# GpSimd takes a subtraction and a product of the query softmax in the first eight units of an attention and token mixer

## The chip, the cores and the metric

The kernel runs on one core of a Trainium2 chip. The metric is the device time of one execution in microseconds (us), as the median of several runs; lower is better. A core has a matrix engine (TensorE, PE in the profile), a vector engine (VectorE, DVE), an activation engine (ScalarE, ACT), a general engine (GpSimd, POOL) and a queue that issues transfers (SyncE, SP). Each runs its own instructions in the order in which they stand in the program, and waits on semaphores for the others.

## The reference, cut to what matters

Shapes: batch 8, 8 heads, 576 positions, head size 64, model size 512, 256 token features, 1536 channel features, all float32.

```python
q_s = exp(q - max(q, axis=-1)); q_s = q_s / (sum(q_s, axis=-1) + 1e-9)
k_s = exp(k - max(k, axis=2));  k_s = k_s / (sum(k_s, axis=2) + 1e-9)
kv  = einsum('bhsd,bhse->bhde', k_s, v)
x   = einsum('bhsd,bhde->bhse', q_s, kv)          # then (batch, 576, 512)
h   = relu(x^T @ w_tok1) @ w_tok2                 # mixes the 576 positions
u   = x + h^T
out = u + relu(u @ w_ch1) @ w_ch2                 # mixes the 512 channels
```

## The kernel before

**Units.** The attention and the token mixing are done in 32 units, one for each batch and each pair of heads (`n = b * 4 + j`). A unit's queries are one tile `q_t` of 128 partitions by 640 (five blocks of 128 positions, the last one half real, by two heads of 64). A unit goes through these steps: `softmax_k` and `softmax_q`; `stage_qT` (transposes of the queries on PE, L340 and L343); `stage_kv` (the product of keys and values, L310); `stage_y` (the queries times the first token weight, L375); `stage_h1` (L383, then `hh` on ACT at L390 and its low half `hl` on DVE at L391); `stage_u` (L428 and L412 on PE, then L416 on ACT and L417 on DVE empty the result).

**Early units.** Units 0 to 7 are "early": they come before the channel mixing starts, and they use tiles of a pool that holds three of each (`q_t` of unit n + 3 takes the place of that of unit n). The channel weights and token weights come as 64-bit numbers, and `narrow` turns each piece of 128 by 512 into float32 with five operations on DVE (L192, L194, L195, L197, L199) and one on ACT (L193); `split` then makes a high half on ACT (L117) and a low half on DVE (L118). That narrowing is the filling work of DVE among the early units: the token weights first, then four pairs of channel pieces.

**The query softmax, before.** DVE takes the maximum of each of the ten rows of 64 in a partition (L278). In units 0 to 3 (and 8 to 11) DVE negates it (L281) and ACT does ten exponentials of 64 with the maximum as bias, each of which also gives its sum (L284). In the other units DVE subtracts the maximum (L288), ACT does one exponential of 640 (L289), and DVE sums (L290). Then DVE adds 1e-9 (L291), takes the reciprocal (L292) and multiplies the whole tile by it (L293). For early units that is the end; late units go on to a high and a low half of the queries, the low one on GpSimd (L118).

**The main part.** From about 81 us on the channel mixing runs: for each of nine blocks of 512 positions, 12 steps of two big products (L488 and L648 on PE), with the late units between them.

**What sets the order.** The code gives the instructions in an order, and the compiler's scheduler then places them by its own estimate of when each engine is free, so that each engine's list is fixed when the program is built. A change to one operation can therefore move many others. Nothing is reordered while it runs.

Of the kernel before, what the change touches and what calls it, by code (L numbers as in the profile page):

```python
# [12 lines left out]
ALU = mybir.AluOpType  # L13
AX = mybir.AxisListType

P = 128
# [4 lines left out]
def attn_mixer_kernel(ctx: ExitStack, tc: tile.TileContext, q, k, kt, v, wt, out, dims):  # L21
# [3 lines left out]
    nc = tc.nc  # L25
    B, H, S, D, TOK, DM, DCH, wide = dims
    NJ = DM // P
# [8 lines left out]
    NE = 2 * NJ  # L36
# [75 lines left out]
    def f32(ap):  # L112
        return ap.bitcast(F32)

    def split(hi, lo, src, lo_eng):

        nc.scalar.copy(hi, src)  # L117
        return lo_eng.tensor_tensor(lo, src, f32(hi), op=ALU.subtract).ins  # L118
# [153 lines left out]

    def softmax_q(u):
        G = 2 * C1
        st = sm.tile([P, 3, G], F32, name="st")
        qc = u["q"]
        qt = qc.rearrange("p c (h d) -> p (c h) d", h=2)
        nc.vector.tensor_reduce(st[:, 0, :], qt, axis=AX.X, op=ALU.max)  # L278
        if u["n"] < NJ or NE <= u["n"] < NE + NJ:

            nc.vector.tensor_scalar(st[:, 0, :], st[:, 0, :], -1.0, None, op0=ALU.mult)  # L281
            for i in range(G):
                one = slice(i, i + 1)
                nc.scalar.activation(  # L284
                    qt[:, i, :], qt[:, i, :], AF.Exp, bias=st[:, 0, one], accum_out=st[:, 1, one]
                )
        else:
            nc.vector.tensor_tensor(qt, qt, st[:, 0, :].unsqueeze(2).broadcast_to([P, G, D]), op=ALU.subtract)  # L288
            nc.scalar.activation(qc, qc, AF.Exp)  # L289
            nc.vector.tensor_reduce(st[:, 1, :], qt, axis=AX.X, op=ALU.add)  # L290
        nc.vector.tensor_scalar(st[:, 1, :], st[:, 1, :], 1e-9, None, op0=ALU.add)  # L291
        nc.vector.reciprocal(st[:, 2, :], st[:, 1, :])  # L292
        nc.vector.tensor_tensor(qt, qt, st[:, 2, :].unsqueeze(2).broadcast_to([P, G, D]), op=ALU.mult)  # L293
        if u["early"]:
            return
        qh = wk.tile([P, C1, P], F32R, name="qh")
        ql = wk.tile([P, C1, P], F32R, name="ql")
        q_low[:] = [split(qh, ql, qc, nc.gpsimd)]

        nc.scalar.copy(qh[TL:P, C, :], f32(ql[TL:P, C, :]))  # L300
        u["qh"], u["ql"] = qh, ql
# [393 lines left out]
    def soft(n):  # L695
        if n < NU:
            softmax_k(units[n])
            softmax_q(units[n])
# [21 lines left out]
    early = early_pools.enter_context(tc.tile_pool(name="early", bufs=NB))  # L720
# [88 lines left out]
    for n in range(NE, NU):  # L809
# [13 lines left out]
        if n + 1 < PAIRED:  # L823
            put(at, lambda n=n: after(drained, softmax_k, units[n + 1]))
            put(at, lambda n=n: after(drained, softmax_q, units[n + 1]))
            put(at + 1, lambda n=n: after(drained + q_low, exp_k, units[n + 1]))
        elif n + 1 < NU:
            put(at, lambda n=n: after(drained, softmax_q, units[n + 1]))
# [15 lines left out]
    n = len(steps)  # L844
# [119 lines left out]
```

## Time and profile before

| what | value |
|---|---|
| time, three runs | 794.89, 797.23, 797.31 us; median 797.23 |
| profiled execution | 798.31 us, of which the span from first to last instruction is 796.5 us |
| mean granted TensorE clock | 0.994 |
| GpSimd work between 2.9 us and 111.6 us | none |

The profile is of one execution. A row of its timeline gives the start, the duration, the engine, the line, the operation and the tiles; consecutive instructions of one kind are merged, with their count. The recorded durations of DVE instructions overlap a little, so what an instruction costs its queue is read from the start of one to the start of the next.

### The profile page before, as it was taken

How to read it: one execution, taken by the hardware profiler on the slowest of the kernel's cores; microseconds unless marked ns; L12 is line 12 of the kernel's file. 1: busy time of each engine (PE TensorE's matmuls, PEld its weight loads, DVE VectorE, ACT ScalarE, POOL GpSimd, SP SyncE). 2: the span in 40 equal slices, each digit the busy share in tenths (PEclk: the TensorE clock that was granted, in tenths of full speed). 3: DMA queues.
4: the chain of work that ended last, by engine and by line, in shares of the span. 5: the costliest groups of instructions: out<-in, count | busy, mean ns of one | idle time of the engine just before them, and what ended most of it. 6: DMA issues, size and time to landing. Idle time of an engine off the chain costs nothing.

```text
span 796.5 us, 12193 instructions
## 1 busy us (share of the span) xinstructions
PE 781.0 (98%) x4478; PEld 651.9 (82%) x4478; DVE 526.9 (66%) x1224; ACT 331.9 (42%) x896; POOL 83.4 (10%) x72
## 2 busy tenths in 40 slices
PE   6899999999999999999999999999999999999997
PEld 5688888888888788888888888888888888888886
DVE  6889999876776445655575555563767458975440
ACT  6977554455643343243433434343434413332100
POOL 1000010011112111020200201111111000000020
PEclk8899999999999999999999999999999999999999
DMA  9754333324334221513132222212240000000011
GB/s 289 236 160 132 105 126 107 107 78 128 87 102 136 65 75 35 152 36 99 39 106 67 80 57 80 92 54 81 51 126 18 1 1 32 22 1 0 1 67 40
DMA packets 64276, 65.10 MB, mean 82 GB/s; under 512 B 41432, under 2 KB 44760, under 8 KB 64216
## 3 DMA queue, kind: packets, MB, share of 16 engines
q1 hardware_dynamic: 59608, 56.06, 23.9%
q10 hardware_dynamic: 4608, 8.26, 2.7%
q8 instruction: 35, 0.57, 0.3%
q14 instruction: 25, 0.20, 0.1%
HBM read 54.85 MB, written 9.45 MB: 81 GB/s over the span
## 4 chain that ended last, share of the span: by engine, by line
PE 94%; DVE 2%; DMA 1%; SPq 1%; ACT 1%; issue 0%; DVEq 0%
PE ps_o L648 33%; PE ps_h L488 29%; PE ps_h L597 7%; PE ps_h L375 6%; PE ps_h L412 6%; PE ps_h L648 4%; PE ps_h L310 2%; PE ps_h L458 2%; PE ps_h L383 2%; DMA kt_t<-in_kt 1%; PE ps_o L375 1%; PE ps_o L412 1%; PE ps_o L428 0%; DVE mc L241 0%; PE ps_h L428 0%; DVE stg L197 0%
## 5 line engine op out<-in xcount | busy, mean ns | idle before, releaser
L648 PE MATMUL ps_o<-h2h,cw 128*128 128x512 f32 x768 | 225.5, 391 | 0.0
L488 PE MATMUL ps_h<-uh,cw 128*128 128x512 f32 x672 | 210.1, 393 | 0.0
L648 PEld LDWEIGHTS ps_o<-h2h,cw 128*128 128x128 f32 x768 | 142.5, 188 | 29.8 <-DVE stg L685 0.5
L492 DVE SCALAR_TENSOR_TENSOR h2l<-ps_h,h2h 128x512 fp32r<-128x512 f32 x84 | 57.8, 689 | 152.6 <-ACT h2h L491 152.6
L488 PEld LDWEIGHTS ps_h<-uh,cw 128*128 128x128 f32 x672 | 123.7, 188 | 24.5 <-issue 0.5
L648 PE MATMUL ps_o<-h2l,cw 128*128 128x512 f32 x384 | 137.3, 391 | 0.0
L488 PE MATMUL ps_h<-ul,cw 128*128 128x512 f32 x336 | 131.0, 390 | 0.0
L648 PEld LDWEIGHTS ps_o<-h2l,cw 128*128 128x128 f32 x384 | 71.9, 188 | 15.3 <-DVE h2l L492 0.3
L118 POOL TENSOR_TENSOR ql<-q_t,qh 128x640 fp32r<-128x640 f32 x24 | 38.2, 1590 | 421.2 <-ACT qh L117 383.6
L491 ACT ACTIVATE h2h<-ps_h 128x512 fp32r<-128x512 f32 x84 | 50.0, 595 | 71.9 <-PE ps_h L488 70.8
L488 PEld LDWEIGHTS ps_h<-ul,cw 128*128 128x128 f32 x336 | 63.1, 188 | 13.4
L362 DVE COPY stack<-cv_s 32x160 f32<-32x160 f32 (+1 forms) x264 | 56.2, 231 | 3.6 <-PE ps_h L458 0.7
L270 POOL TENSOR_TENSOR k_t<-k_t,mb 128x640 f32<-128x640 f32 x24 | 38.2, 1590 | 119.4 <-DMA mb<-row 83.3
L271 ACT ACTIVATE k_t<-k_t 128x640 f32<-128x640 f32 x24 | 17.8, 741 | 72.1 <-POOL k_t L270 70.7
L506 DVE TENSOR_TENSOR ul<-ps_h,ul 128x512 f32<-128x512 f32 x40 | 27.5, 692 | 24.2 <-PE ps_h L597 23.9
L416 ACT CAST uh<-ps_h 128x128 fp32r<-128x128 f32 (+4 forms) x104 | 27.6, 288 | 30.7 <-PE ps_h L458 20.2
L362 ACT COPY stack<-cv_s 32x128 f32<-32x128 f32 (+1 forms) x120 | 36.9, 308 | 2.8 <-DVE cv_s L352 1.5
L417 DVE TENSOR_TENSOR ul<-ps_h,uh 128x128 fp32r<-128x128 f32 (+4 forms) x104 | 30.8, 312 | 6.0 <-ACT uh L416 5.1
L412 PE MATMUL ps_h<-w2h,hh 128*128 128x320 f32 (+1 forms) x112 | 33.7, 302 | 0.0
L412 PE MATMUL ps_h<-w2l,hh 128*128 128x320 f32 (+1 forms) x112 | 33.1, 298 | 0.0
L648 PE MATMUL ps_h<-cw 128*128 128x512 f32 x144 | 33.0, 389 | 0.0
L412 PE MATMUL ps_h<-w2h,hl 128*128 128x320 f32 (+1 forms) x112 | 32.6, 298 | 0.2 <-DVE hl L391 0.2
(249 smaller groups left out, 1283.8 us busy)
## 6 DMA issues: line engine op xcount, KB each, us to landing
stg<-in_w SPq DMA_DIRECT2D x28, 512.0 KB, 4.2
kt_t<-in_kt SPq DMA_DIRECT2D x32, 320.0 KB, 2.9
q_t<-in_q SPq DMA_DIRECT2D x32, 320.0 KB, 3.4
k_t<-in_k SPq DMA_DIRECT2D x24, 320.0 KB
out<-stg ACTq DMA_DIRECT2D x27, 256.0 KB, 2.0
v_t<-in_v SPq DMA_DIRECT2D x46, 128.0 KB, 2.7
part<-in_v SPq DMA_DIRECT2D x18, 128.0 KB, 2.5
mb<-row SPq DMA_DIRECT2D x23, 64.0 KB, 3.0
```

What stands on the lines that cost most here:

```text
L118: return lo_eng.tensor_tensor(lo, src, f32(hi), op=ALU.subtract).ins
L270: nc.gpsimd.tensor_tensor(kx, kx, mb.unsqueeze(1).broadcast_to([P, C1, P]), op=ALU.subtract)
L362: eng(stack[row : row + Q, h, 0:n, at : at + Q], turned[x * Q : (x + 1) * Q, 0:n, y * Q : (y + 1) * Q])
L375: nc.tensor.matmul(y[:, 0:TOK], a, w, start=(i == 0), stop=(i == len(mm) - 1))
L412: nc.tensor.matmul(to, a, w, start=start and i == 0, stop=stop and i == len(mm) - 1)
L416: nc.scalar.copy(uh, src).ins,
L417: nc.vector.tensor_tensor(ul, src, f32(uh), op=ALU.subtract).ins,
L488: nc.tensor.matmul(t, cw[f][x][:, n, :], w, start=(i == 0), stop=(i == 3 * NJ - 1))
L491: nc.scalar.activation(hh, t, AF.Relu).ins,
L492: nc.vector.scalar_tensor_tensor(hl, t, 0.0, f32(hh), op0=ALU.max, op1=ALU.subtract).ins,
L597: nc.tensor.matmul(t, x(n), w[n], start=(n == 0 and i == 0), stop=(n == 1 and i == 2))
L648: nc.tensor.matmul(to, cw[f][x][:, n0 + n, :], w, start=(first and i == 0), stop=(last and i == 2))
```

## The change

`softmax_q` gets an engine by name. For early units the subtraction of the maximum and the product by the reciprocal sums go to GpSimd; for late units they stay on DVE. And among the early units only unit 0 keeps the ten small exponentials: units 1, 2 and 3 now take the other branch (subtract, one exponential of 640, sum).

```diff
     def softmax_q(u):
         G = 2 * C1
+        eng = nc.gpsimd if u["early"] else nc.vector
         st = sm.tile([P, 3, G], F32, name="st")
...
-        if u["n"] < NJ or NE <= u["n"] < NE + NJ:
+        if u["n"] == 0 or NE <= u["n"] < NE + NJ:
...
         else:
-            nc.vector.tensor_tensor(qt, qt, st[:, 0, :].unsqueeze(2).broadcast_to([P, G, D]), op=ALU.subtract)
+            eng.tensor_tensor(qt, qt, st[:, 0, :].unsqueeze(2).broadcast_to([P, G, D]), op=ALU.subtract)
             nc.scalar.activation(qc, qc, AF.Exp)
             nc.vector.tensor_reduce(st[:, 1, :], qt, axis=AX.X, op=ALU.add)
         nc.vector.tensor_scalar(st[:, 1, :], st[:, 1, :], 1e-9, None, op0=ALU.add)
         nc.vector.reciprocal(st[:, 2, :], st[:, 1, :])
-        nc.vector.tensor_tensor(qt, qt, st[:, 2, :].unsqueeze(2).broadcast_to([P, G, D]), op=ALU.mult)
+        eng.tensor_tensor(qt, qt, st[:, 2, :].unsqueeze(2).broadcast_to([P, G, D]), op=ALU.mult)
```

The first added line moves every later line of the code down by one: L288 is L289 in the changed kernel, L293 is L294, L391 is L392. Lines before it (L192 to L241, L118) keep their numbers.

How the lists of instructions move is seen at three places. On GpSimd, the difference between the two lists after the last fill of the start (rows with + are new; `L289` is the subtraction, `L294` the product; the last row is the first of the late units):

```order
 L60 MEMSET v_t 64x130
+L294 TENSOR_TENSOR q_t<-q_t,st 128x640
+L289 TENSOR_TENSOR q_t<-q_t,st 128x640 x2
+L294 TENSOR_TENSOR q_t<-q_t,st 128x640 x2
+L289 TENSOR_TENSOR q_t<-q_t,st 128x640 x2
+L294 TENSOR_TENSOR q_t<-q_t,st 128x640 x2
+L289 TENSOR_TENSOR q_t<-q_t,st 128x640 x2
+L294 TENSOR_TENSOR q_t<-q_t,st 128x640
+L289 TENSOR_TENSOR q_t<-q_t,st 128x640
+L294 TENSOR_TENSOR q_t<-q_t,st 128x640 x2
 L118 TENSOR_TENSOR ql<-q_t,qh 128x640
```

Fifteen instructions have come to an engine that had none there: the product of unit 0, then the subtractions of units 1 to 7 and the products of units 1 to 7.

On DVE, around the product of unit 3, before (`q_t_439` and `st_455` are the queries and sums of unit 3, `st_555` those of unit 4; `hl_512` is the low half of unit 1):

```order
L199 TENSOR_TENSOR cv_s_328<-stg_326,cv_s_328 128x128
L291 TENSOR_SCALAR st_455<-st_455 128x10
L292 RECIPROCAL st_455<-st_455 128x10
L293 TENSOR_TENSOR q_t_439<-q_t_439,st_455 128x640
L391 SCALAR_TENSOR_TENSOR hl_512<-ps_h_508,hh_511 128x256
L290 TENSOR_REDUCE st_555<-q_t_539 128x10
L278 TENSOR_REDUCE st_647<-q_t_631 128x10
```

And of the change (`st_439` are the sums of unit 3, `st_531` those of unit 4; the low half of unit 1 stands eight rows ahead of this piece):

```order
L291 TENSOR_REDUCE st_531<-q_t_515 128x10
L418 TENSOR_TENSOR ul0_104<-ps_h_399,uh0_100 128x320
L292 TENSOR_SCALAR st_439<-st_439 128x10
L197 SCALAR_TENSOR_TENSOR stg_789<-stg_789 128x512
L194 SCALAR_TENSOR_TENSOR cv_s_802<-stg_800,cv_s_802 128x512
L292 TENSOR_SCALAR st_531<-st_531 128x10
L293 RECIPROCAL st_439<-st_439 128x10
L418 TENSOR_TENSOR ul0_104<-ps_o_491,uh0_100 128x320
L199 TENSOR_TENSOR cv_s_791<-stg_789,cv_s_791 128x512
```

The product has gone from the list, the reciprocal that GpSimd waits for has two steps of the weight narrowing (L197, L194) ahead of it, and another (L199) follows.

On DVE again, ahead of the low half of unit 6, before (`hl_987`; `stg_1012` and `stg_1023` are pieces of channel weight):

```order
L194 SCALAR_TENSOR_TENSOR cv_s_1025<-stg_1023,cv_s_1025 128x512
L195 TENSOR_SCALAR stg_1023<-stg_1023 128x512
L118 TENSOR_TENSOR cw0_117<-cv_s_1014,cw0_117 128x4x128
L417 TENSOR_TENSOR ul1_105<-ps_o_905,uh1_101 128x320
L197 SCALAR_TENSOR_TENSOR stg_1023<-stg_1023 128x512
L417 TENSOR_TENSOR ul1_105<-ps_h_915,uh1_101 128x128
L391 SCALAR_TENSOR_TENSOR hl_987<-ps_o_983,hh_986 128x256
```

And of the change (`hl_963` is the low half of unit 6; `stg_1050` is the last of the eight channel pieces, of which nothing was narrowed ahead of this place before):

```order
L197 SCALAR_TENSOR_TENSOR stg_1050<-stg_1050 128x512
L316 TENSOR_SCALAR rs_946<-ps_o_935 128x1
L118 TENSOR_TENSOR cw0_117<-cv_s_1041,cw0_117 128x4x128
L418 TENSOR_TENSOR ul1_105<-ps_h_891,uh1_101 128x128
L199 TENSOR_TENSOR cv_s_1052<-stg_1050,cv_s_1052 128x512
L317 RECIPROCAL rs_946<-rs_946 128x1
L392 SCALAR_TENSOR_TENSOR hl_963<-ps_o_959,hh_962 128x256
```

Weight narrowing stands ahead of this low half that stood behind it before. Counted over the whole list up to this row, DVE has 12 fewer rows of `q_t<-q_t,st` and three fewer of L281, three more sums (L290), and 13 more rows of narrowing: two each of L118, L192, L194, L195 and L197, and three of L199.

## The prediction

> **What bounds the kernel now.** I read the page first, then the stretches of the span, then PE's waits.
>
> ```profile
> PE 781.0 (98%) x4478; PEld 651.9 (82%) x4478; DVE 526.9 (66%) x1224; ACT 331.9 (42%) x896; POOL 83.4 (10%) x72
> PE 94%; DVE 2%; DMA 1%; SPq 1%; ACT 1%; issue 0%; DVEq 0%
> core 0: us, PE busy (x) PEld busy (x) DVE busy (x) ACT busy (x) POOL busy (x), PEclk, DMA share, GB/s
> 0.00:80.00 80.00, 69.10 (x512) 59.36 (x513) 68.02 (x172) 61.09 (x199) 2.15 (x17) 0.94 0.65 203
> 80.00:797.00 717.00, 711.88 (x3968) 592.57 (x3966) 458.87 (x1053) 270.78 (x698) 81.25 (x55) 1.00 0.23 68
> 12.49:79.88 67.39, 59.63 (x443) 50.51 (x439) 63.13 (x161) 52.77 (x171) 0.00 (x0) 0.92 0.61 194
> ```
>
> PE is busy for 98% of the span and makes 94% of the chain. After 80 us it rests for 5 us of 717, so the main part costs its PE work and no more. Whatever the change does, it does in the first 80 us, where PE rests for 10.9 us, and an idle us that is added there is added to the time. Between 12.49 us (the first load that DVE waits for behind the start) and 79.88 us DVE rests for only 67.39 - 63.13 = 4.3 us: it is as full as PE. GpSimd does nothing there.
>
> PE's waits before 82 us, the longest, and the only one after it:
>
> ```profile
> PE ps_h L248 <- ACT kt_t L245: 3.9, 2, 3.2
> PE ps_o L383 <- ACT ys L377: 2.1, 1, 2.1
> PE ps_h L375 <- ACT w1f L214: 0.9, 1, 0.9
> PE ps_h L310 <- DVE h2l L492: 0.6, 1, 0.6
> ```
>
> **What the change takes away and adds.**
>
> ```profile
> L293 DVE TENSOR_TENSOR q_t<-q_t,st 128x640 f32<-128x640 f32 x8 | 6.6, 827 | 0.1
> L288 DVE TENSOR_TENSOR q_t<-q_t,st 128x640 f32<-128x640 f32 x4 | 3.3, 825 | 0.0
> L284 ACT ACTIVATE q_t<-q_t,st 128x64 f32<-128x64 f32 x40 | 13.5, 342 | 1.2 <-DVE st L281 1.0
> L289 ACT ACTIVATE q_t<-q_t 128x640 f32<-128x640 f32 x4 | 3.0, 738 | 1.8 <-DVE q_t L288 1.8
> L118 POOL TENSOR_TENSOR ql<-q_t,qh 128x640 fp32r<-128x640 f32 x24 | 38.2, 1590 | 421.2 <-ACT qh L117 383.6
> ...
> 109.58 0.82 DVE L293 TENSOR_TENSOR q_t<-q_t,st 128x640 f32<-128x640 f32 x1
> 110.32 0.69 DVE L679 TENSOR_TENSOR part<-ps_o,uh 128x512 f32<-128x512 f32 x1
> 115.63 0.42 DVE L195 TENSOR_SCALAR stg<-stg 128x512 uint32<-128x512 uint32 x1
> 115.97 0.42 DVE L192 TENSOR_SCALAR cv_s<-stg 128x512 uint32<-128x512 uint32 x1
> ```
>
> The last four rows give what an instruction costs its queue, start to start: a product of 640 takes 0.74 us, a narrowing step of one input (L192, L195) 0.34. Two-input steps of 512 are 0.60 apart (111.52 to 112.12, below), sums of 640 are 0.73 apart (593.31 to 594.04).
>
> DVE loses 8 products and 4 subtractions, 12 x 0.74 = 8.9 us, and three negations (0.2); it gains three sums, 3 x 0.73 = 2.2. By the rows of the order, the scheduler fills the gap with 13 rows of narrowing ahead of the low half of unit 6: 9 x 0.60 + 4 x 0.34 = 6.8 us. So ahead of that row DVE has 8.9 + 0.2 - 2.2 - 6.8 = **0.1 us** less work than before: the freed time is spent, on weights that PE doesn't yet wait for.
>
> ACT loses three times ten exponentials of 0.34 us (3.4) for three of 0.74: 3 x 2.7 = 8 us. Before, that sat in front of `ys` and `w1f` (waits of 2.1 and 0.9 us above).
>
> GpSimd gains 15 operations on two inputs in SBUF. The kind is shown by its L118: 1.59 us on the mean, 1.56 at the least. What such an operation does to DVE is shown at four places:
>
> ```profile
> 111.52 0.69 DVE L194 SCALAR_TENSOR_TENSOR cv_s<-stg,cv_s 128x512 uint32<-128x512 uint32 x1
> 111.60 2.03 POOL L118 TENSOR_TENSOR ql<-q_t,qh 128x640 fp32r<-128x640 f32 x1 [108.72 <-ACT qh L117]
> 112.12 2.06 DVE L118 TENSOR_TENSOR cw<-cv_s,cw 128x512 fp32r<-128x512 f32 x1
> 114.10 0.68 DVE L492 SCALAR_TENSOR_TENSOR h2l<-ps_h,h2h 128x512 fp32r<-128x512 f32 x1
> ...
> 149.69 1.70 POOL L270 TENSOR_TENSOR k_t<-k_t,mb 128x640 f32<-128x640 f32 x1 [36.07 <-ACT mb L265]
> 149.89 2.05 DVE L197 SCALAR_TENSOR_TENSOR stg<-stg 128x512 f32<-128x512 uint32 x1
> ...
> 351.52 1.57 POOL L118 TENSOR_TENSOR ql<-q_t,qh 128x640 fp32r<-128x640 f32 x1 [11.14 <-ACT qh L117]
> 351.92 0.69 DVE L492 SCALAR_TENSOR_TENSOR h2l<-ps_h,h2h 128x512 fp32r<-128x512 f32 x1 [0.47 <-ACT h2h L491]
> ...
> 593.22 1.56 POOL L270 TENSOR_TENSOR k_t<-k_t,mb 128x640 f32<-128x640 f32 x1 [9.18 <-DMA mb<-row]
> 593.31 0.81 DVE L278 TENSOR_REDUCE st<-q_t 128x10 f32<-128x640 f32 x1
> 594.04 0.81 DVE L241 TENSOR_REDUCE dg<-kt_t 128x1 f32<-128x640 f32 x1
> ```
>
> At 111.60 GpSimd starts while DVE is in a two-input step, and is 0.47 us longer than its 1.56. DVE's next two-input step then takes 2.06 us instead of 0.69 and ends when GpSimd has ended: they shut each other out for a whole instruction. At 149.89 the same, 2.05 us. A DVE step that reads one input from PSUM (351.92) and a reduction (593.31) go on beside it undisturbed. Before, this cost the kernel nothing, since GpSimd first works at 111.6 us; now 15 such operations stand in the one stretch where DVE has no slack.
>
> I went through DVE's list behind each of the fifteen. The product of unit 0 falls into DVE's wait for a load: nothing. Behind eight (subtractions of units 1, 2, 3, 6, 7, products of 1, 5, 6) a shut-out step is next or next but one: 8 x 1.56 = 12.5 us. Behind the other six DVE first has work that goes on: 0.7 us (a reduction) behind the products of 2 and 4, leaving 0.85 each; 0.3 to 0.45 (steps out of PSUM) behind the subtraction of 4, the products of 3 and 7 and the subtraction of 5, leaving 1.2, 1.2, 1.1 and 1.3. Sum 12.5 + 6.5 = **19.0 us**. No row shows the one-input steps L192 and L195 beside GpSimd. Bounds: they go on like the reduction (four times 0.34 us less, 17.6) or are shut out; I take shut out, since at 0.34 us for 512 elements against 0.60 they read twice as fast as the steps that are. For the whole sum the ends are 12 us (every operation finds 0.75 us of other work) and 21.8 (14 x 1.56).
>
> The Trainium skill, SBUF, section Who interferes with whom, calls it an exclusive lock on ports that DVE and GpSimd share, held for a whole instruction, and counts one-input steps in a two-port mode among those shut out, reductions never. With that, 19.0; without the one-input steps 17.6; the trace agrees as far as it shows them.
>
> **The sum**, taken where PE last waits for DVE among the early units, at the low half of unit 6:
>
> ```profile
> 78.03 0.61 PE L383 MATMUL ps_h<-kvf,ys 128*128 128x128 f32 x4
> 78.41 0.42 DVE L391 SCALAR_TENSOR_TENSOR hl<-ps_o,hh 128x256 fp32r<-128x256 f32 x1
> 79.42 0.31 PE L412 MATMUL ps_h<-w2h,hl 128*128 128x320 f32 x1
> 80.48 0.31 PE L412 MATMUL ps_o<-w2h,hh 128*128 128x320 f32 x1
> ```
>
> DVE reaches L391 of unit 6 at 78.41. With -0.1 of work, +19.0 of shut-outs and at best all of its 4.3 us of rest used up, it comes 14.6 us later. Before, the result (78.41 + 0.42 = 78.83) lay 0.6 us until PE took it at 79.42; that cover goes: 14.0. And in PE's new order L384 and L429 of unit 7 (four and four passes, from 78.03 and before, 1.4 us) stand behind unit 6's products instead of ahead: **+15.4 us** when PE is as far as it was at 80.48. After that PE never rests, so nothing is won back, and nothing more lost: unit 7's low half has 4 us of channel products ahead of it.
>
> A mid-point: the product of unit 3.
>
> ```profile
> 38.61 0.82 DVE L293 TENSOR_TENSOR q_t<-q_t,st 128x640 f32<-128x640 f32 x1
> 40.23 0.60 PE L340 MATMUL ps_o<-ident,q_t 128*128 128x128 f32 x4
> 44.16 0.61 PE L383 MATMUL ps_o<-kvf,ys 128*128 128x128 f32 x4
> ```
>
> It ended at 39.4 and PE took it at 40.23. Now the maximum, subtraction (1.56), exponential (0.74), sum and product (1.56) pass through three queues, with narrowing ahead of the reciprocal; laid end to end with the shut-outs I get the product's end at about 50 us. All that PE had done before by 44.16, bar unit 3's own part, it can still do by about then; then it rests for some 5 us.
>
> What PE's rest does to its clock:
>
> ```profile
> 32.00:33.00 1.00, 1.00 (x9) 0.67 (x7) 0.52 (x1) 0.99 (x4) 0.00 (x0) 0.65 0.12 46
> 33.00:34.00 1.00, 1.00 (x19) 1.00 (x20) 1.00 (x4) 0.63 (x3) 0.00 (x0) 0.50 0.61 169
> 35.00:36.00 1.00, 1.00 (x6) 0.94 (x5) 1.00 (x4) 1.00 (x8) 0.00 (x0) 0.64 1.02 358
> ```
>
> After the wait of 2.1 us for `ys` the granted clock is at half from 32.3 to 35.7 us, 1.7 us lost. While PE waits for DVE a slow clock costs nothing; behind the last rest it may cost up to 1.7 us more. I leave it out and keep it for the upper end. (The Trainium skill, TensorE: Matmul & The Clock Gate, Part 1, has a window of about 3.4 us that decides on half or full clock; 3.4 us is what the rows give.)
>
> The sum stands against the profiled execution: 798.3 + 15.4 = 813.7. That execution lay 1.1 us over the median of the three runs, so I say **812.5 us**.
>
> **Rivals.**
>
> *No shutting out, and only moved waits.* If GpSimd disturbed DVE little, PE would gain the 2.1 and 0.9 us that ACT's exponentials caused, and lose them again at unit 3's product (two times 1.56 instead of 0.74, about 3 us of rest at 39 us): 797 to 799, no change that can be measured. For it: DVE has 0.1 us less work. Against: the rows at 112.12 and 149.89. Chance 0.08.
>
> *ACT's relief carries through: faster.* The same, but the queue of unit 3 holds no new rest. 798.3 - 3.0 - 0.9 (half of the slow clock at 32 us) = 794.4, on the median's scale 793.3. It decides if the shut-outs stay below DVE's 4.3 us of rest. Against: that would be 0.3 us for each of 14, where the rows show 1.4. Chance 0.04.
>
> *The shut-outs are half hidden.* If DVE finds much more to do beside GpSimd, or its rests lie just there, 12 us of shut-outs give 15.4 - 7 = 8.4; if the narrowing moved ahead also slips behind what PE waits for, 3 to 8. I give 800 to 805 a chance of 0.10.
>
> *More than the sum.* Slow clock behind the last rest, DVE rests that stay (its loads wait for PE, which is late), 21.8 instead of 19.0: 817 to 823. Chance 0.10.
>
> **How the numbers follow.** Forecast, 805 to 817: 0.68. With the rivals that is slower in 0.68 + 0.10 + 0.10 = 0.88, within 0.3% (2.4 us, about what a measurement of this kernel can tell from no change) 0.08, faster 0.04. The range 801 to 819 leaves out both small rivals, a fifth of the low one and half of the high one, some 0.2.
>
> **What would show it.** In the changed profile: two-input steps of DVE (L194, L197, L199, L118) of 2 us or so before 80 us, and fourteen GpSimd operations of which many last over 1.56; DVE busy nearly without a gap from 13 to 95 us, by its records; PE's waits before 100 us naming POOL `q_t` L294 and DVE `hl` L392; the first channel product (L489) some 15 us later than now; the stretch after it as long as before. The prediction is wrong if DVE's steps keep 0.69 us beside GpSimd, or if PE's rest before the first L489 doesn't grow by 10 us or more; the step to doubt first is that all of DVE's lateness reaches PE.

## The result, and the profile after

| kernel | runs | median, us | lowest to highest |
|---|---|---|---|
| before | 4 | 796.66 | 794.89 to 797.31 |
| after | 4 | 807.88 | 805.98 to 808.28 |

The ratio after to before is 1.014 (95% interval 1.0116 to 1.0164): the change makes the kernel 11.2 us slower. Predicted were 812.5 us, 801 to 819. The profiled execution of the changed kernel took 805.98 us (span 803.7), the quickest of its four and 7.7 us above the profiled execution of before (798.31). So 3.5 us of the 11.2 are not in these two profiles; the other three executions of the changed kernel, 1.7 to 2.3 us longer, show a mean granted clock of 0.992 where this one shows 0.994.

Two rows of the page of the changed kernel, the engines' busy time and the chain that ends last:

```profile
PE 783.4 (97%) x4478; PEld 654.3 (81%) x4478; DVE 531.8 (66%) x1212; ACT 323.4 (40%) x839; POOL 105.4 (13%) x87
...
PE 90%; DVE 7%; DMA 1%; ACT 1%; issue 1%; POOL 0%; DVEq 0%; ACTq 0%; SPq 0%; POOLq 0%
```

DVE has twelve instructions fewer and is busy 4.9 us longer. Its share of the chain rose from 2% to 7%. By stretches of the span (in order: PE, PEld, DVE, ACT, POOL busy, then granted clock, DMA share, GB/s):

```profile
0.00:80.00 80.00, 64.43 (x457) 55.31 (x457) 72.05 (x155) 51.17 (x133) 24.35 (x32) 0.94 0.68 203
80.00:803.00 723.00, 718.97 (x4023) 598.97 (x4022) 459.74 (x1058) 272.18 (x707) 81.00 (x55) 1.00 0.22 68
```

PE has 64.4 us busy in the first 80 where it had 69.1, and rests for 15.6 instead of 10.9. The same columns up to the first channel product (L488 at 81.02 us before, L489 at 88.71 now), and from 12.49 us to the low half of unit 6; before stands first in each pair:

```profile
0.00:81.02 81.02, 70.12 (x521) 60.38 (x521) 69.04 (x174) 62.08 (x201) 2.15 (x17) 0.94 0.64 201
0.00:88.71 88.71, 72.10 (x516) 61.92 (x517) 80.02 (x174) 56.54 (x148) 24.35 (x32) 0.94 0.63 189
...
12.49:78.41 65.92, 58.16 (x433) 49.10 (x429) 61.66 (x157) 51.59 (x168) 0.00 (x0) 0.92 0.63 198
12.49:85.86 73.37, 59.95 (x447) 50.43 (x447) 72.54 (x157) 46.57 (x114) 20.46 (x14) 0.93 0.61 183
```

The first channel product comes 7.7 us later, and PE rests 16.6 us ahead of it instead of 10.9, which is 5.7 more. From there to the end of the span it is 715.0 us, where it was 715.5. Up to the low half of unit 6, DVE rests 0.8 us, where it had 4.3. What PE waits for ahead of 110 us, the longest rows:

```profile
PE ps_o L341 <- POOL q_t L294: 6.4, 3, 4.5
PE ps_o L248 <- ACT kt_t L245: 2.8, 1, 2.8
PE ps_h L248 <- ACT kt_t L245: 1.9, 2, 1.0
PE ps_h L376 <- DVE rs L317: 1.7, 1, 1.7
...
PE ps_h L413 <- DVE hl L392: 1.0, 1, 1.0
```

Both waits that the prediction named are there: GpSimd's product and the low half. In the timeline of the changed kernel, GpSimd's operations and the DVE step beside each (start, length, engine, line):

```profile
20.45 1.37 POOL L289 TENSOR_TENSOR q_t<-q_t,st 128x640 f32<-128x640 f32 x1 [4.94 <-DVE st L279]
20.69 1.16 DVE L292 TENSOR_SCALAR st<-st 128x10 f32<-128x10 f32 x1
...
45.00 1.26 POOL L294 TENSOR_TENSOR q_t<-q_t,st 128x640 f32<-128x640 f32 x1 [5.68 <-DVE st L293]
45.12 1.68 DVE L199 TENSOR_TENSOR cv_s<-stg,cv_s 128x512 f32<-128x512 f32 x1
46.31 0.77 PE L341 MATMUL ps_o<-ident,q_t 128*128 128x128 f32 x4 [4.51 <-POOL q_t L294]
...
55.92 1.82 POOL L289 TENSOR_TENSOR q_t<-q_t,st 128x640 f32<-128x640 f32 x1 [4.33 <-DVE st L279]
56.69 1.34 DVE L192 TENSOR_SCALAR cv_s<-stg 128x512 uint32<-128x512 uint32 x1
...
85.86 0.40 DVE L392 SCALAR_TENSOR_TENSOR hl<-ps_o,hh 128x256 fp32r<-128x256 f32 x1
86.32 0.41 PE L413 MATMUL ps_h<-w2h,hl 128*128 128x320 f32 x1 [1.04 <-DVE hl L392]
88.71 0.81 PE L489 MATMUL ps_h<-uh,cw 128*128 128x512 f32 x2
```

A two-input step that takes 0.69 us takes 1.68; one-input steps are shut out as well, a narrowing step of 512 (0.42 alone, 1.34 here) and even one of ten elements (0.17 alone, 1.16 here). GpSimd's operation takes 1.26 us where nothing disturbs it, not 1.56. Unit 3's product ends at 46.26, and PE takes it at 46.31 after a rest of 4.5 us; unit 6's low half comes at 85.86, 7.4 us later than before.

What the shut-outs cost can be read row by row: the recorded length of a DVE step less its usual length. Fourteen of the fifteen operations have such a step: 0.22, 1.05, 0.99, 1.06, 0.59, 1.06, 0.93, 0.99, 0.66, 0.73, 0.91, 1.06, 0.98 and 0.93 us, in order of time. The sum is **12.2 us**; the prediction had 19.0. This sum is called the excess below.

### The profile page after: what moved, and what is told of

The parts are those of the page before. It is cut to its first block, busy times and chain, and to the rows that moved or that the text cites. A ratio compares the mean times of both kernels' runs of the same rounds, so it can differ in the third digit from the quotient of the medians.

```text
span 803.7 us, 12153 instructions
## 1 busy us (share of the span) xinstructions
PE 783.4 (97%) x4478; PEld 654.3 (81%) x4478; DVE 531.8 (66%) x1212; ACT 323.4 (40%) x839; POOL 105.4 (13%) x87
## 4 chain that ended last, share of the span: by engine, by line
PE 90%; DVE 7%; DMA 1%; ACT 1%; issue 1%; POOL 0%; DVEq 0%; ACTq 0%; SPq 0%; POOLq 0%
PE ps_o L649 33%; PE ps_h L489 29%; PE ps_h L598 7%; PE ps_h L376 6%; PE ps_h L413 5%; PE ps_h L649 4%; PE ps_h L459 2%; PE ps_h L311 2%; PE ps_h L384 1%; DVE cv_s L194 1%; DVE stg L197 1%; DMA kt_t<-in_kt 1%; DVE cv_s L199 1%; DVE mc L241 1%; DVE st L291 1%
## 5 line engine op out<-in xcount | busy, mean ns | idle before, releaser
L489 PE MATMUL ps_h<-uh,cw 128*128 128x512 f32 x672 | 210.8, 393 | 0.0
L489 PEld LDWEIGHTS ps_h<-uh,cw 128*128 128x128 f32 x672 | 123.8, 188 | 24.7 <-issue 0.5
L489 PE MATMUL ps_h<-ul,cw 128*128 128x512 f32 x336 | 131.0, 390 | 0.0
L118 POOL TENSOR_TENSOR ql<-q_t,qh 128x640 fp32r<-128x640 f32 x24 | 38.2, 1591 | 364.3 <-ACT qh L117 325.3
L489 PEld LDWEIGHTS ps_h<-ul,cw 128*128 128x128 f32 x336 | 63.1, 188 | 13.3
```

The costliest lines, as they stand in the source:

```text
L489: nc.tensor.matmul(t, cw[f][x][:, n, :], w, start=(i == 0), stop=(i == 3 * NJ - 1))
```

## The experiments

Three theories were set against each other. Theory 1: GpSimd's two-input operations shut DVE out where it has no slack. Theory 2: the chain of maximum, subtraction, exponential, sum and product has become longer, and PE waits for that, whoever is shut out. Theory 3: the whole exponentials, and the order that the scheduler makes with them, cost the time, and GpSimd nothing. All medians are of 4 to 12 runs, each beside its own runs of the kernel before; "excess" is the sum just explained, for the first 95 us of the profiled execution.

| kernel | median, us | ratio to before (95% interval) | excess, us |
|---|---|---|---|
| after | 807.88 | 1.014 (1.0116 to 1.0164) | 12.2 |
| whole exponentials alone | 803.24 | 1.0074 (1.006 to 1.0089) | 0 |
| the same, and 15 operations beside the path | 811.24 | 1.0176 (1.016 to 1.0193) | 12.4 |
| the same, with two whole inputs | 815.16 | 1.0229 (1.0211 to 1.0246) | 15.8 |
| the same, one input read | 805.72 | 1.0107 (1.0089 to 1.0124) | 5.0 |
| the same, write only | 803.02 | 1.0078 (1.0062 to 1.0094) | 1.4 |
| GpSimd alone, ten-part exponentials kept | 804.34 | 1.0092 (1.0077 to 1.0108) | 6.4 |
| after, GpSimd for unit 3 only | 801.90 | 1.0055 (1.0039 to 1.007) | 0.7 |
| after, GpSimd for all but unit 3 | 810.13 | 1.0168 (1.0151 to 1.0186) | 11.2 |
| after, memsets for GpSimd's operations | 801.64 | 1.0055 (1.0037 to 1.0073) | 1.0 |
| the same, without the memsets | 795.68 | 0.9979 (0.9971 to 0.9987) | 0 |
| ten-part exponentials for eight units | 803.80 | 1.0087 (1.007 to 1.0105) | 0 |
| ten-part exponentials for five units | 798.47 | 1.0014 (1.0005 to 1.0023) | 0 |

### Whole exponentials alone

```diff
-        if u["n"] < NJ or NE <= u["n"] < NE + NJ:
+        if u["n"] == 0 or NE <= u["n"] < NE + NJ:
```

GpSimd gets nothing; both operations stay on DVE.

> Theory 1 (GpSimd's products and subtractions shut DVE out, some 12 us in all in the profile of the changed kernel, in the stretch where DVE has no slack): without GpSimd, DVE only gains three subtractions and three sums (4.4 us) and loses three negations (0.2); of its 4.3 us of rest most is used up: 796 to 800 us, DVE's steps of 512 at their usual 0.69. Theory 2 (the longer chain of maximum, subtraction, exponential, sum and product to unit 3's product, for which PE rests 4.5 us after the change): the chain gets only a sum and a subtraction longer, 797 to 800. Theory 3 (the whole exponentials and the order that the scheduler makes of them cost the time, GpSimd nothing): 805 to 809, like the changed kernel.

Measured 803.24 us, 5.9 above before: between what theories 1 and 2 expected and what theory 3 did. Alone, this half of the change costs about half of what the whole costs. The stretch 12.5 to 80 us, of before and then of this kernel (columns as above):

```profile
12.50:80.00 67.50, 59.74 (x442) 50.62 (x439) 63.24 (x161) 52.88 (x172) 0.00 (x0) 0.92 0.61 194
```

```profile
12.50:80.00 67.50, 57.30 (x430) 47.59 (x429) 64.03 (x158) 44.64 (x108) 0.00 (x0) 0.90 0.63 192
```

Its longest waits of PE ahead of 110 us:

```profile
PE ps_h L248 <- ACT kt_t L245: 3.2, 2, 2.6
PE ps_h L412 <- ACT w2h L117: 3.0, 1, 3.0
PE ps_h L375 <- DVE w1f L199: 2.2, 1, 2.2
```

ACT is 8.2 us less busy and PE gains nothing by it: the wait for `ys` (2.1 us before) is gone, and in its place PE waits for the narrowed token weights, 2.2 us for `w1f` out of DVE and 3.0 for `w2h`, whose copy on ACT comes behind DVE's narrowing. DVE's subtractions and sums (4.4 us for three units) stand ahead of that narrowing.

Waiting is not the whole of the 5.9 us. From 12.5 us to the first channel product, of before and then of this kernel:

```profile
12.50:81.02 68.52, 60.77 (x451) 51.64 (x447) 64.26 (x163) 53.86 (x174) 0.00 (x0) 0.93 0.60 191
12.50:83.44 70.94, 60.74 (x450) 50.53 (x448) 67.13 (x165) 47.29 (x115) 0.00 (x0) 0.90 0.61 184
```

PE's rests grow from 7.75 to 10.2 us, and by the same 2.4 the first channel product is later. The other 2.9 of the 5.3 us between the two spans (796.5 and 801.8) come behind it, where PE has 16 more products left to do (3976 instead of 3960). Why it has them left wasn't followed up.

### Fifteen operations beside the path

```diff
+    def beside(row):
+        x = spare.rearrange("p (g d) -> p g d", g=2 * C1)
+        nc.gpsimd.tensor_tensor(x, x, row.unsqueeze(2).broadcast_to([P, 2 * C1, D]), op=ALU.mult)
...
         nc.vector.tensor_reduce(st[:, 0, :], qt, axis=AX.X, op=ALU.max)
+        if u["early"] and u["n"] > 0:
+            beside(st[:, 0, :])
...
         nc.vector.reciprocal(st[:, 2, :], st[:, 1, :])
+        if u["early"]:
+            beside(st[:, 2, :])
```

On top of whole exponentials alone; `spare` is 128x640 of the tile `part`, idle in that stretch.

> Same rows in the same order on PE, DVE, ACT and SP as the kernel with whole exponentials alone; GpSimd does 15 operations of the changed kernel's form on a spare tile at the moments where the changed kernel has them, and nobody waits for a result of theirs. Theory 1: DVE steps of 512 beside them last up to 1.7 us, some 10 to 12 us in all, and PE is 8 to 12 us later than with whole exponentials alone: 805 to 811 us. Theories 2 and 3: a result that nobody waits for costs nothing, within 1.5 us of whole exponentials alone.

Measured 811.24, 8.0 us above whole exponentials alone, by operations whose results nobody uses and with every other engine's list unchanged. This is theory 1 by itself, a shade above its range. From the page of the run with whole exponentials alone, the engines' busy time:

```profile
PE 785.3 (98%) x4478; PEld 654.6 (82%) x4478; DVE 530.2 (66%) x1227; ACT 324.8 (41%) x839; POOL 83.2 (10%) x72
```

And with the fifteen beside it:

```profile
PE 785.2 (97%) x4478; PEld 653.0 (81%) x4478; DVE 543.0 (67%) x1227; ACT 323.8 (40%) x839; POOL 106.8 (13%) x88
```

One place of its timeline:

```profile
37.59 1.31 POOL L277 TENSOR_TENSOR part<-part,st 128x640 f32<-128x640 f32 x1 [4.12 <-DVE st L284]
37.69 1.75 DVE L120 TENSOR_TENSOR w2l<-cv_s,w2h 128x512 fp32r<-128x512 f32 x1
39.36 0.81 DVE L284 TENSOR_REDUCE st<-q_t 128x10 f32<-128x640 f32 x1
```

PE is busy as long in both (785.3 and 785.2 us), so what is added is rest. The same 1227 instructions of DVE take 12.8 us longer, nearly all of it the excess of 12.4. A full shut-out costs 1.06 us (1.75 less 0.69) by an operation of 1.26 to 1.31: 0.2 less than the operation lasts. And 8.0 of the 12.4 us reach the time, not all.

### The same with two whole inputs, with one input, and with none

```diff
-        nc.gpsimd.tensor_tensor(x, x, row.unsqueeze(2).broadcast_to([P, 2 * C1, D]), op=ALU.mult)
+        nc.gpsimd.tensor_tensor(x, x, row, op=ALU.mult)              # x of 128x10, in all three
+        nc.gpsimd.tensor_tensor(a, a, b, op=ALU.mult)                # first: a, b of 128x640
+        nc.gpsimd.tensor_scalar(a, a, 0.5, None, op0=ALU.mult)       # second
+        nc.gpsimd.memset(spare, 0.5)                                 # third: 128x1280
```

> As the kernel with 15 operations beside the path, but both inputs are whole (128x640 each), as in the two-input operations from which the prediction took its 1.56 us, with an operation of 128x10 ahead that reads the row. If a row of ten read 64 times over is why the changed kernel's operations last 1.26 us, these last 1.56 undisturbed and shut DVE out 0.3 us longer each: DVE's busy time 4 us above that of the run with 1.26, and the time 813 to 816 us. If the length has another reason: 810 to 813.

> As the kernel with 15 operations beside the path, same rows in the same order on PE, DVE, ACT and SP; GpSimd's operation is one of 128x10 that reads the row and a product of 128x640 by a constant, so that it reads one input of SBUF and not two. If only a second input shuts DVE out: within 2 us of whole exponentials alone, 801 to 805 us, as with the memsets. If any reading of SBUF does: DVE's steps beside it last until it has ended, and the time is 809 to 813.

> As the kernel with 15 operations beside the path, same rows in the same order on PE, DVE, ACT and SP, but GpSimd's operation is split into one of 128x10 that reads the row and a memset of 128x1280 (about 1.2 us) that reads nothing. If what DVE is shut out by is GpSimd's reading of two inputs from SBUF: within 2 us of whole exponentials alone (801 to 805 us). If any access of GpSimd to SBUF shuts DVE out for as long as it lasts: 809 to 813 as with the two-input operations. DVE's steps beside the memsets show it directly: 0.69 or 1.7 us.

Two whole inputs: 815.16 us, an operation is 1.55 us long undisturbed, a full shut-out costs 1.34, and the excess is 15.8, 3.4 above that with 1.26 us (DVE's busy time alone rose by 2.1). Writing only: 803.02, the same as without. One input: 805.72, in between and outside both ranges that had been expected. The timelines, in that order:

```profile
15.18 2.16 DVE L297 TENSOR_TENSOR q_t<-q_t,st 128x640 f32<-128x640 f32 x1
...
26.35 1.55 POOL L278 TENSOR_TENSOR part<-part 128x640 f32<-128x640 f32 x1
```

```profile
47.95 1.81 POOL L278 TENSOR_SCALAR part<-part 128x640 f32<-128x640 f32 x1
48.02 1.20 DVE L196 SCALAR_TENSOR_TENSOR cv_s<-stg,cv_s 128x512 uint32<-128x512 uint32 x1
```

```profile
45.46 1.17 POOL L278 MEMSET part<- 128x1280 f32 x1
45.98 0.68 DVE L196 SCALAR_TENSOR_TENSOR cv_s<-stg,cv_s 128x512 uint32<-128x512 uint32 x1
...
55.49 1.17 POOL L278 MEMSET part<- 128x1280 f32 x1
55.55 1.39 DVE L194 TENSOR_SCALAR cv_s<-stg 128x512 uint32<-128x512 uint32 x1
```

What two-input steps of DVE are shut out by is GpSimd's reading: beside a memset the step at 45.98 keeps its 0.68 us. Why reading one input costs so much less than reading two (an excess of 5.0 against 15.8 us), no run shows. A one-input step can be shut out by a memset too (0.42 alone, 1.39 at 55.55). The Trainium skill, SBUF — State Buffer, section Who interferes with whom, makes the same two distinctions: two SBUF inputs contend with a GpSimd instruction that reads, not with one that only writes, and one-input steps in a two-port mode contend with any. The rows agree with the first; for the second they show the shut-out, and not in which mode the steps ran.

### Unit 3 alone, and all but unit 3

```diff
-        eng = nc.gpsimd if u["early"] else nc.vector
+        eng = nc.gpsimd if u["n"] == 3 else nc.vector                  # first
+        eng = nc.gpsimd if u["early"] and u["n"] != 3 else nc.vector   # second
```

> The changed kernel with GpSimd for unit 3 alone. Theory 1: DVE loses 1.5 us of work and is shut out for 2: within 2 us of whole exponentials alone. Theory 2: unit 3's product is what PE rests 4.5 us for after the change, so most of the loss is here: 803 to 808 us. Theory 3: 805 to 809 as whole exponentials alone.

> The changed kernel with unit 3's two operations back on DVE. Theory 1: thirteen of the fifteen operations stay, with 10 of 12 us of shut-outs: 804 to 808 us. Theory 2: the chain to unit 3's product is that of whole exponentials alone: 797 to 801. Theory 3: 805 to 809.

Measured 801.90 and 810.13. Theory 2 in the form that unit 3's product through GpSimd is the loss falls: with it alone the time is no worse than with whole exponentials alone (803.24; the intervals of the ratios overlap), and without it no better than the changed kernel. The second lies above every range that had been expected. Why it doesn't help to take unit 3 back shows in the timeline of the second, at the one early product that DVE has there:

```profile
41.75 0.81 DVE L291 TENSOR_REDUCE st<-q_t 128x10 f32<-128x640 f32 x1
...
46.88 0.22 DVE L293 RECIPROCAL st<-st 128x10 f32<-128x10 f32 x1
47.00 0.77 DVE L294 TENSOR_TENSOR q_t<-q_t,st 128x640 f32<-128x640 f32 x1
...
47.88 1.08 PE L341 MATMUL ps_o<-ident,q_t 128*128 128x128 f32 x4 [7.00 <-ACT uh L417]
```

The product is DVE's again and takes 0.77 us, but it begins at 47.00: the last sum is done at 42.6, and the reciprocal comes at 46.88, behind low halves and narrowing in DVE's list. PE rests 7.0 us ahead of it.

### GpSimd alone

The change's lines with `eng`, but the condition of before (`u["n"] < NJ or ...`): 8 products and 4 subtractions on GpSimd, ten-part exponentials for units 0 to 3.

> The kernel before with its 8 products and 4 subtractions of the early units on GpSimd, and the exponentials of units 1 to 3 still by ten parts. If the two parts of the change add up (whole exponentials alone 6 us, the changed kernel 11): 800 to 804 us. Theory 1 alone, from DVE's work: 12 operations taken away (8.9 us) against 12 shut-outs of 0.8 on the mean (9.8), with what the scheduler puts in the gap on top: 797 to 803. Theory 2 (moved waits only): 796 to 798.

Measured 804.34, 7.8 above before: a little over what the sum by theory 1 allowed (797 to 803), far above theory 2's 796 to 798. The two halves alone cost 5.9 and 7.8, together 13.7, and both at once 11.2: they overlap somewhat and don't cancel.

### The lock taken out of the changed kernel, then the length too

```diff
-            eng.tensor_tensor(qt, qt, st[:, 0, :].unsqueeze(2).broadcast_to([P, G, D]), op=ALU.subtract)
+            late_only(u, st[:, 0, :])
...
+    def late_only(u, row):
+        qc = u["q"]
+        nc.gpsimd.tensor_tensor(qc[:, 0, 0 : 2 * C1], qc[:, 0, 0 : 2 * C1], row, op=ALU.mult)
+        nc.gpsimd.memset(qc, 0.5)      # not in the second kernel
+        nc.gpsimd.memset(qc, 0.5)      # not in the second kernel
```

The product likewise, for the early units: both kernels leave out the subtraction and the product there.

> The changed kernel with each of GpSimd's fifteen operations replaced by one of 128x10 that reads the same row and two memsets of q's tile (about 0.4 + 0.6 + 0.6 us): the subtraction and the product of the early units are left out, and what follows waits for GpSimd as long as before or longer, while GpSimd hardly reads. (The scheduler's order differs from the changed kernel's at some places, and cannot be held the same.) Theory 1 (shut-outs): some 11 of 12 us of excess in DVE's steps go, and with them 7 to 10 us: 797 to 801 us. Theory 2 (the slower chain through GpSimd): 807 to 811, no better than the changed kernel. Theory 3 (whole exponentials and the scheduler's order, without the shut-outs): 803, as whole exponentials alone, although DVE has 11 us less work.

> As the kernel with memsets, without the memsets: GpSimd has only an operation of 128x10 for each of the fifteen (0.4 us), so that neither the lock nor the longer chain is there, and DVE has 11 us less work than with whole exponentials alone; the subtraction and the product of the early units are left out. (The order differs from the changed kernel's at some places.) If what the kernel with memsets still loses against the kernel before (5 us) is the longer chain through GpSimd, for which PE rests 4 us there: 796 to 798 us. If it is the scheduler's order around the whole exponentials: 801 to 803.

Measured 801.64 and 795.68, the first between the ranges of theories 1 and 3, the second just below that for the chain. With GpSimd in the chain for about as long as in the changed kernel but hardly reading, 6.3 us of the 11.2 go; without the length too, another 6.4 (each beside its own runs of the kernel before), and the kernel is 1.5 us faster than before. The busy row of the first:

```profile
PE 785.3 (98%) x4478; PEld 655.5 (82%) x4478; DVE 519.4 (65%) x1212; ACT 324.2 (41%) x839; POOL 108.1 (14%) x117
```

Its GpSimd operations in the view of groups (count, then busy us and mean ns of one), and PE's longest wait:

```profile
L277 POOL MEMSET q_t<- 128x640 f32 x15 | 10.0, 670 | 0.8
L276 POOL MEMSET q_t<- 128x640 f32 x15 | 9.9, 661 | 0.9
L275 POOL TENSOR_TENSOR q_t<-q_t,st 128x10 f32<-128x10 f32 x15 | 5.2, 344 | 39.7 <-ACT cv_s L193 7.7 <-DVE st L301 5.7 <-DVE st L302 5.6
```

```profile
PE ps_o L353 <- POOL q_t L277: 4.2, 3, 2.5
```

The same wait in the second:

```profile
PE ps_o L351 <- POOL q_t L275: 0.9, 1, 0.9
```

So both theories 1 and 2 hold a part. DVE has 7.5 us less to do in the first kernel than before (526.9 to 519.4), PE waits 4.2 us for GpSimd, and the time is still 5 us longer. That wait is not these 5 us by itself: from 12.5 us to the first channel product (at 84.10) PE rests 8.4 us in all, only 0.6 more than before, since other waits of before are gone. That the longer chain costs the time rests on the second kernel, from which only the memsets are missing. The split isn't exact. GpSimd's three operations there last 0.34 + 0.66 + 0.67 = 1.7 us against 1.26 in the changed kernel, so the 6.4 is rather too much for the chain and the 6.3 rather too little for the lock; and the scheduler, which goes by its own estimate of an operation's length, orders some rows otherwise in each.

### More on ACT in place of more on DVE

```diff
-        if u["n"] < NJ or NE <= u["n"] < NE + NJ:
+        if u["n"] < NE + NJ:                                   # first: eight early units
+        if u["n"] < NJ + 1 or NE <= u["n"] < NE + NJ:          # second: five
```

On the kernel before, without GpSimd.

> The opposite of whole exponentials: the kernel before with the ten exponentials with their sums on ACT for units 4 to 7 too, so that DVE loses four subtractions and four sums (5.9 us) before the channel products begin and ACT gains 4 times 2.7 us (10.8). If DVE's work is what counts there (three units the other way cost 6 us): 791 to 795 us. If ACT becomes what PE waits for: 799 to 805. If neither: 796 to 798.

> The kernel before with the ten exponentials on ACT for unit 4 too: DVE has 1.5 us less work, ACT 2.7 more; one step between the kernel before (four units in ten parts) and that with eight, which was 7 us slower. If the loss there is ACT's load: 797 to 799. If DVE's work counts and ACT has room for one more unit: 794 to 796, better than both kernels. If any other order than that before costs some 4 us: 800 to 802.

Measured 803.80 and 798.47. The first's stretch 12.5 to 80 us:

```profile
12.50:80.00 67.50, 58.43 (x428) 48.38 (x423) 56.32 (x152) 60.94 (x244) 0.00 (x0) 0.92 0.60 184
```

DVE is 6.9 us less busy there than before and ACT 8.1 us more, PE is 1.3 us less busy, and the kernel is slower by 7.3. A new rest of PE stands behind ACT well after that stretch, the only one between 140 and 200 us:

```profile
165.55 1.20 PE L648 MATMUL ps_o<-h2h,cw 128*128 128x512 f32 x4 [1.54 <-ACT h2h L491]
```

Where the other 4 us come from wasn't followed up. That ACT's load turns the balance fits, and is not shown. One more unit (five) is 0.14% slower, hardly to be told from no change. No kernel here that computes the whole result is faster than the one before.

## Why the prediction was right, and which term was off

**Direction and mechanism** held. PE rests longer in the first 80 us (by 4.7), the main part is unchanged (715.5 and 715.0 us), steps of two inputs last up to 1.75 us beside GpSimd, and the run with fifteen operations beside the path shows that this alone costs 8 us with nothing else changed. The rival that put the shut-outs at nothing (797 to 799) is refuted by that run; so, by the time itself, is the one by ACT's relief. With whole exponentials alone ACT had 8 us less to do, and PE waited for DVE's narrowing instead; with neither shut-outs nor chain ("the same, without the memsets" in the table) the kernel gained 1.5 us, where that rival had 3.9.

**A sign that failed.** The prediction called itself wrong if PE's rest before the first L489 didn't grow by 10 us or more, and looked for that product some 15 us later. The rest grew by 5.7, and the product came 7.7 us later. So the way in which the time is lost was right, and its size on the profiled execution about half of what was forecast; that the median still lies within 801 to 819 is owed to a wide range. The slow clock that the prediction kept for the upper end did not come: from 80 us on, the granted clock is 1.00.

**The term that was mis-sized** is the sum of the shut-outs, 19.0 us, which measured 12.2. Two errors make it up. The prediction took 1.56 us for GpSimd's operation, from rows whose second input is a whole tile; the change's second input is a row of ten, repeated, and the operation takes 1.26. The runs with the one and the other kind show 3.4 us of excess between them. And it charged DVE the whole length of the operation, where the full shut-outs cost 1.06 by 1.26 and 1.34 by 1.55, some 0.2 less. The prediction's own row of before showed it: 2.06 us for a step of 0.69 is 1.37, not 1.56. For fourteen operations the two come to 14 x 0.3 + 14 x 0.2 = 7 us; 19.0 - 7 = 12. That this meets the 12.2 so closely is partly luck: the product of unit 5 shut nothing out, where the prediction had 1.56 (DVE waits for a load there until 58.59), while the six operations with a reduced charge cost 4.8 us, not the 3.5 that the two corrections leave of 6.5. The prediction's low end of 12 us does not count for it either: that stood for DVE finding other work (by its own figures 14 x (1.56 - 0.75) = 11.3), not for shorter shut-outs. The choice to take the one-input steps as shut out was right.

With 12.2 in place of 19.0 the prediction's sum reads -0.1 + 12.2 - 4.3 - 0.6 + 1.4 = +8.6 on the profiled execution, 806.9 us; that execution took 805.98. Up to the low half of unit 6 the terms give -0.1 + 12.2 - 4.3 = 7.8 us, and it came 7.4 later: DVE had 1.0 us less work instead of 0.1, and used up 3.4 of its 4.3 us of rest. The median of the changed kernel lies 1.9 us above its profiled execution, so on medians the sum is 2.6 us short.

**The step to doubt first**, that all of DVE's lateness reaches PE, was indeed too simple: beside the path, 8.0 of 12.4 us arrived (and 12.8 of 15.8 with two whole inputs, each beside its own runs of before).

**What the sum left out** is the chain through GpSimd as a cost of its own. The prediction had it as a mid-point, and it was near for the rest (some 5 us; measured 4.5), though the product ended earlier (about 50 us; measured 46.26). But it was not said that with the shut-outs nearly gone such a rest would still be there: the kernel with memsets waits 4.2 us for GpSimd and is 5 us slower than before. The two costs stand beside each other, and taking away the one leaves the other. Nor did the prediction say that whole exponentials alone would cost 5.9 us; it had them only as 4.4 us of DVE's work set off against the operations given away.

**Open** remains how much of the loss with whole exponentials alone is DVE's work and how much the scheduler's other order (an order held fixed wasn't tried), what part of the 6.4 us between the last two variants of the changed kernel is the chain itself, and what the 3.5 us are by which the medians differ more than the two profiled executions.

## What to carry to other kernels

Before an elementwise operation goes from DVE to GpSimd, count what DVE does beside it: here each full shut-out cost DVE 1.06 us, more than the 0.74 that the operation had cost DVE itself. Price a shut-out by what a recorded step exceeds its usual length, and by a row with the same kinds of operands, not by the length of the operation that causes it. And where two engines are both nearly full ahead of a third, try the move in both directions: here work moved to DVE and work moved to ACT each cost 6 to 7 us.

## What the runs showed of the hardware

- GpSimd's product of 128x640 takes 1.26 us when the second input is a row of ten repeated 64 times each, 1.55 when it is a whole tile, and 1.81 or more when it is a constant and only one input is read.
- That one-input operation, though the longest, holds a DVE step back by at most 0.5 us (1.20 instead of 0.68 at 48.02, while it lasts from 47.95 to 49.76). The whole-instruction lock that the Trainium skill, SBUF — State Buffer, section Who interferes with whom, describes is borne out by the two-input operations (1.06 by 1.26) and not by this one.
- A DVE step on ten elements is shut out about as long as one on 512 (0.17 to 1.16 us at 20.69 in the changed kernel, 0.42 to 1.34 at 56.69).
